# The first projection of an attention and two feed-forward networks in seven block products instead of eight, for the later token tiles

## The chip, the cores and the metric

The kernel runs on one core of a Trainium2 chip. The metric is the device time of one launch in microseconds (us). The core has a matrix engine (TensorE, PE in the rows; its weight loads are PEld), a vector engine (VectorE, DVE), a scalar engine (ScalarE, ACT), a general engine (GpSimd, POOL) and SyncE (SP), which issues most of the transfers here.

## The reference

Three stages follow one another on 6016 tokens with 256 channels.

```
qn = q / |q| over tokens;  kn = k / |k| over tokens
a  = softmax(kn^T qn / tau)                  # 256 x 256, over channels
x  = v a                                     # 6016 x 256
h  = x w_in                                  # 6016 x 2048
g  = h where h >= 1; 0 where h <= -1; (h+1)^2 / 4 between
x  = g w_out                                 # 6016 x 256
xn = x / sqrt(mean(x^2) + 1e-6) * rms_g
y  = (silu(xn w_gate) * (xn w_val)) w_out    # inner width 1536
```

The weights come as 64-bit numbers, the tokens as 32-bit ones, and the output is 32-bit.

## The kernel before

**Precision.** Each operand of the large products is split into a high and a low part (tiles ending in h and l). A product of two blocks of 128 x 128 weights and 128 x 512 tokens is three matmuls: high by high, low by high and high by low.

**Tiles.** The tokens lie in 12 tiles, in six pairs: five pairs of 512 columns a tile and a last one of 448. Tiles stand transposed, channels on the partitions. The attention matrix is folded into the weights: w1 = a w_in is made once (`product_w1`) and kept in SBUF as w1h and w1l.

**First network.** `block_A` makes one block of 128 rows of h for one tile: two halves of the channels by three matmuls, six matmuls into one PSUM bank, 16 blocks a tile. Then come three ScalarE instructions (relu, square, copy to the high part) and two on VectorE (clamp, subtraction to the low part). `block_B` multiplies them by w_out into y, which grows in PSUM over the 16 blocks. `prep_v` turns and splits V for one tile.

**Second network.** `norm` scales x. `combine` makes the seven operands of Strassen's method in Winograd's form from a pair of tiles (two tiles by two channel halves): b11, b21, b22 and the differences t1 to t4. `to_seven` makes the seven weight blocks of a panel, which is two row blocks by two channel halves, and stores them in DRAM; `load_seven` fetches a panel (896 KB). `seven_units` makes the seven products of a panel and a pair, 21 matmuls where the plain way has 24. Its PSUM sum X1 grows over four of the products and is copied out three times on the way (names ending in a, c and u); three VectorE additions complete the sums. `block_D` multiplies by the second w_out.

**Order.** `ORDER` says in which order the networks of the pairs run: first network of pairs 0 and 1, second of pair 0, first of pair 2, second of pair 1, and so on; the second networks of pairs 4 and 5 end it. A string, `CHAIN`, lays out a panel's products (c), those left over from the panel before (t) and the waiting products of the projection that follows (d). A planner written in Python then sorts every operation by a due time, with assumed costs, and gives out buffers by class (`SLOTS`); on each engine the program then keeps that order. Its clock starts where the first block of h is computed, near 62 us on the trace. The transfers are issued from SP's queue in the planner's order too.

Of the kernel before, what the change touches and what calls it, by code (L numbers as in the profile page):

```python
# [62 lines left out]
def tile_channel_attention_two_ffn(  # L63
# [422 lines left out]
    n_op = {cls: SLOTS[cls] for cls in ("stage", "op", "rows")}  # L486
    first_op = {"stage": 0, "op": n_op["stage"], "rows": n_op["op"] + n_op["stage"]}
# [7 lines left out]
    class Buf:  # L495
        def __init__(self, cls, name, shape=None, dtype=F32, slot=None):
            self.cls, self.name, self.shape, self.dtype = cls, name, shape, dtype
            self.slot, self.t, self.users, self.given = slot, None, 0, None
            self.wrote, self.read = {}, {}

# [53 lines left out]
    for t in range(2):  # L554
        V[t] = [Buf("op", f"v{p}{t}", slot=2 * t + i) for i, p in enumerate("hl")]
# [4 lines left out]
    def prep_v(t, at, step):  # L560
        _, n = tiles[t]
        x = Buf("stage", f"vin{t}", [P, NC, TOK])
# [15 lines left out]
    def narrow(key, src, at, step, on_act, into=None):  # L578
        x = Buf("stage", f"wide_{key}", [P, NC, TOK])
# [32 lines left out]
    for p in range(NF2 // 2):  # L612
        kept_dram["wd", p] = drp.tile([P, 4 * C], F32, name=f"kept_wd{p}")
        for nm in "gv":
            kept_dram[nm, p] = drp.tile([P, 2, 7, P], F32, name=f"kept_{nm}{p}")

    def to_rows(kind, j, src, at, step, on_act, eng):
        x = narrow(f"{kind}{j}", src, at, step, on_act)
        w = Buf("rows", f"{kind}{j}", [P, 2, 2, C], F32R)
# [14 lines left out]
    def to_seven(kind, p, src, at, step):  # L634
        f = Buf("stage", f"f{kind}{p}", [P, 8, P])
        h = Buf("stage", f"h{kind}{p}", [P, 7, P], F32R)
        narrow(f"{kind}{p}", src, at, step, True, f)
        for i, (o, a, b, how) in enumerate((
# [9 lines left out]
            at, [(f, s) for s in range(1, 8)], [h], [h])  # L648
# [48 lines left out]
    G, Y = {}, {}  # L697

    def block_A(t, f, at):
        _, n = tiles[t]  # L700
        vh, vl = V[t]
        ps = Buf("mm", f"h{t}_{f}")

        def mm():
# [9 lines left out]
        op("PE", pe(6, n), mm, at, reads, [ps], [ps])  # L714
        r = Buf("tmp", f"g{t}_{f}")
        gh = Buf("tmp", f"gh{t}_{f}", dtype=F32R)
        op("ACT", act(n), lambda: nc.scalar.activation(  # L717
            out=r.t[:, :n], in_=ps.t[:, :n], func=AF.Relu, bias=0.5, scale=0.5),
            at, [ps], [r], [r])
# [3 lines left out]
            out=r.t[:, :n], in0=ps.t[:, :n], scalar=1.0, in1=r.t[:, :n], op0=ALU.max, op1=ALU.min),  # L723
            at, [ps], [r])
        op("ACT", act(n), lambda: nc.scalar.activation(  # L725
            out=gh.t[:, :n], in_=r.t[:, :n], func=AF.Copy), at, [r], [gh], [gh])
        gl = Buf("tmp", f"gl{t}_{f}", dtype=F32R)
# [4 lines left out]
    def block_B(t, f, c, w, at):  # L732
        _, n = tiles[t]
        gh, gl = G[t, f]
        if (f, c) == (0, 0):
# [517 lines left out]
```

## Time and profile before

| what | value |
|---|---|
| median of 3 runs | 1135.0 us (1134.12 to 1135.71) |
| profiled execution, its own time | 1134.83 us |
| its span, first to last instruction | 1133.1 us |
| busy: PE, DVE, ACT, POOL | 1109.2, 820.0, 749.6, 86.4 us |
| bytes moved by DMA | 167.65 MB |

The profile is of one execution. A busy time is the time in which an engine had an instruction under way. Matmuls are pipelined, so the printed durations of neighbours overlap, and what one costs is read from the distance of two starts. The same holds, to a lesser degree, for VectorE and ScalarE.

### The profile page before, as it was taken

Reading aid. Unit: us, or ns where it says so; the run is one execution under the profiler, and the core shown is the slowest. Engines: PE = TensorE matmul, PEld = TensorE weight load, DVE = VectorE, ACT = ScalarE, POOL = GpSimd, SP = SyncE. Lnnn points to the kernel's source line nnn. Section 1 sums busy time; section 2 is a strip of 40 time slices with the busy share of each in tenths; the row PEclk is TensorE's granted clock in tenths of the full one; section 3 lists DMA queues with packets and bytes.
Section 4 is the critical chain, followed back from the end, with each engine's and each line's share of the span. In section 5 each row is a group of like instructions: output and inputs, shape, how many; then the busy total and the mean of one; then the engine's idle time right before and its main releaser. Section 6 shows DMA issues by size and latency. Waiting matters only on the chain.

```text
span 1133.1 us, 13952 instructions
## 1 busy us (share of the span) xinstructions
PE 1109.2 (98%) x4950; PEld 930.7 (82%) x4950; DVE 820.0 (72%) x1311; ACT 749.6 (66%) x1325; POOL 86.4 (8%) x84
## 2 busy tenths in 40 slices
PE   7799999999999999999999999999999999999996
PEld 6678888888888888888888888888888998888995
DVE  5989989969985448886446977445968545976664
ACT  6589898987666666666666556666557566555552
POOL 0000244313100002000000100000200000200000
PEclk9999999999999999999999999999999999999998
DMA  9766575577536413425432432532442412444742
GB/s 346 238 174 180 189 258 217 196 201 260 163 115 185 80 56 135 155 97 123 124 75 102 167 135 53 183 63 89 149 167 103 126 56 92 161 153 155 216 149 33
DMA packets 138854, 167.65 MB, mean 148 GB/s; under 512 B 103712, under 2 KB 103712, under 8 KB 138784
## 3 DMA queue, kind: packets, MB, share of 16 engines
q1 hardware_dynamic: 135072, 166.29, 47.2%
q10 hardware_dynamic: 3712, 0.46, 0.3%
q8 instruction: 39, 0.64, 0.2%
q14 instruction: 31, 0.25, 0.1%
HBM read 142.21 MB, written 24.51 MB: 147 GB/s over the span
## 4 chain that ended last, share of the span: by engine, by line
PE 93%; DMA 4%; DVE 1%; SPq 1%; ACT 0%; issue 0%; DVEq 0%; ACTq 0%
PE y L742 23%; PE h L708 22%; PE o L948 17%; PE vx L855 9%; PE gx L855 9%; PE gy L855 4%; PE vy L855 4%; PE vz L855 2%; PE gz L855 2%; DMA qk<-in_k_dram 1%; DMA wide<-in_moe_w_in_dram 1%; DMA qk<-in_q_dram 1%; PE w_ps L682 1%; SPq L180 1%; DMA soon<-in_moe_w_out_dram 1%; PE w_ps L405 0%
## 5 line engine op out<-in xcount | busy, mean ns | idle before, releaser
L722 DVE SCALAR_TENSOR_TENSOR g<-h,g 128x512 f32<-128x512 f32 (+1 forms) x192 | 129.1, 676 | 144.9 <-ACT g L720 144.9
L742 PE MATMUL y<-gh,wo 128*128 128x512 f32 (+1 forms) x768 | 233.5, 385 | 0.0
L717 ACT ACTIVATE g<-h 128x512 f32<-128x512 f32 (+1 forms) x192 | 112.8, 587 | 121.5 <-PE h L708 121.3
L948 PE MATMUL o<-uh,wd 128*128 128x512 f32 (+1 forms) x576 | 175.6, 386 | 0.0
L742 PEld LDWEIGHTS y<-gh,wo 128*128 128x128 f32 x768 | 144.2, 188 | 27.3 <-DVE wo L143 0.2
L708 PE MATMUL h<-vh,w1h 128*128 128x512 f32 (+1 forms) x384 | 148.1, 386 | 0.3 <-ACT w1h L414 0.3
L708 PE MATMUL h<-vl,w1h 128*128 128x512 f32 (+1 forms) x384 | 148.0, 385 | 0.3 <-DVE vl L143 0.3
L742 PE MATMUL y<-gl,wo 128*128 128x512 f32 (+1 forms) x384 | 148.0, 385 | 0.1
L143 DVE TENSOR_TENSOR gl<-g,gh 128x512 fp32r<-128x512 f32 (+1 forms) x192 | 129.2, 678 | 7.4 <-ACT gh L725 7.1
L948 PEld LDWEIGHTS o<-uh,wd 128*128 128x128 f32 x576 | 108.1, 188 | 20.4
L720 ACT ACTIVATE g<-g 128x512 f32<-128x512 f32 (+1 forms) x192 | 119.0, 621 | 4.2
L725 ACT ACTIVATE gh<-g 128x512 fp32r<-128x512 f32 (+1 forms) x192 | 117.0, 611 | 6.8 <-DVE g L722 6.8
L708 PE MATMUL h<-vh,w1l 128*128 128x512 f32 (+1 forms) x384 | 116.8, 385 | 0.0
L948 PE MATMUL o<-ul,wd 128*128 128x512 f32 (+1 forms) x288 | 111.2, 386 | 1.5 <-DVE ul L143 1.5
L708 PEld LDWEIGHTS h<-vh,w1h 128*128 128x128 f32 x384 | 72.1, 188 | 14.6 <-ACT w1h L414 0.7
L708 PEld LDWEIGHTS h<-vl,w1h 128*128 128x128 f32 x384 | 72.1, 188 | 14.2 <-DVE vl L143 0.6
L742 PEld LDWEIGHTS y<-gl,wo 128*128 128x128 f32 x384 | 72.1, 188 | 13.7 <-DVE gl L143 0.4
L708 PEld LDWEIGHTS h<-vh,w1l 128*128 128x128 f32 x384 | 72.1, 188 | 13.6 <-DVE w1l L415 0.3
L948 PEld LDWEIGHTS o<-ul,wd 128*128 128x128 f32 x288 | 54.1, 188 | 12.1 <-DVE ul L143 1.9
L855 PE MATMUL gy<-xt,gw 128*128 128x512 f32 (+1 forms) x216 | 60.0, 386 | 0.0
L855 PE MATMUL vx<-xt,vw 128*128 128x512 f32 (+1 forms) x216 | 60.0, 386 | 0.0
L855 PE MATMUL gx<-xb,gw 128*128 128x512 f32 (+1 forms) x216 | 60.0, 386 | 0.0
(181 smaller groups left out, 1840.1 us busy)
## 6 DMA issues: line engine op xcount, KB each, us to landing
gw<-kept_g SPq DMA_DIRECT2D x36, 896.0 KB, 4.7
vw<-kept_v SPq DMA_DIRECT2D x36, 896.0 KB, 4.7
wo<-kept_wo SPq DMA_DIRECT2D x40, 512.0 KB, 4.0
wd<-kept_wd SPq DMA_DIRECT2D x36, 512.0 KB, 3.6
vin<-in_v_dram SPq DMA_DIRECT2D x80, 64.0 KB, 3.9
out_dram<-ob SPq DMA_DIRECT2D x80, 64.0 KB, 2.0
qk<-in_q_dram SPq DMA_DIRECT2D x9, 512.0 KB, 10.2
qk<-in_k_dram SPq DMA_DIRECT2D x9, 512.0 KB, 10.2
```

Source lines behind the costliest of these rows:

```text
L143: return eng.tensor_tensor(out=dst_lo, in0=src, in1=hi.bitcast(F32), op=ALU.subtract)
L180: nc.sync.dma_start(out=xv[32 * a:32 * a + 32, c, :n // 32, :], in_=src[a, c])
L682: nc.tensor.matmul(got[b].t, x[:, c * P:(c + 1) * P], w[:, c, :], start=(i == 0), stop=(i == len(terms) - 1),)
L708: nc.tensor.matmul(ps.t[:, :n], w[:, c, f * P:(f + 1) * P], x[:, c, :n], start=(i == 0), stop=(i == len(terms) - 1),)
L717: op("ACT", act(n), lambda: nc.scalar.activation(out=r.t[:, :n], in_=ps.t[:, :n], func=AF.Relu, bias=0.5, scale=0.5), at, [ps], [r], [r])
L720: op("ACT", act(n), lambda: nc.scalar.activation(out=r.t[:, :n], in_=r.t[:, :n], func=AF.Square), at, [], [r])
L722: op("DVE", dve(n), lambda: nc.vector.scalar_tensor_tensor(out=r.t[:, :n], in0=ps.t[:, :n], scalar=1.0, in1=r.t[:, :n], op0=ALU.max, op1=A ...
L725: op("ACT", act(n), lambda: nc.scalar.activation(out=gh.t[:, :n], in_=r.t[:, :n], func=AF.Copy), at, [r], [gh], [gh])
L742: nc.tensor.matmul(y.t[:, c, :n], w.t[:, f % 2, h, cs], x[:, :n], start=(f == 0 and i == 0), stop=(f == NF1 - 1 and i == 2),)
L855: nc.tensor.matmul(ps.t[:, :n], w.t[:, h, a, :], b.t[:, e, :n], start=(start and i == 0), stop=(i == 2), skip_group_check=True,)
L948: nc.tensor.matmul(o.t[:, c, :n], w.t[:, f % 2, h, cs], x[:, :n], start=(nth == 1 and i == 0), stop=(nth == NF2 and i == 2),)
```

## The change

From pair 2 on, the first projection is made by `seven_units` too. Its panels of weights (kind h) are made from w1h + w1l, eight of them, stored in DRAM, and loaded for each pair. V is turned into a plain 32-bit tile and goes through `combine`. The instructions behind a block of h are taken out of `block_A` into `squared`, which reads either PSUM or an SBUF sum. Pairs 0 and 1 stay as they were. The stream class has four buffers in place of three. The class stage is merged into op. CHAIN has another order. The core of the diff:

```diff
-CHAIN = "ccttccddcdd"
-SLOTS = {"mm": 4, "yo": 2, "stage": 7, "op": 19, "rows": 4, "tmp": 20, "seven": 3}
-RESERVE = {"tmp": 4, "mm": 1}
+CHAIN = "cttccdcdcdd"
+CHAIN_1 = "cdttccddcddcddd"
+PLAIN = 2
+H_AT = (70.0, 16.0)
+PREP_S = 50.0
+SLOTS = {"mm": 4, "yo": 2, "op": 24, "rows": 4, "tmp": 20, "seven": 4}
+RESERVE = {"tmp": 4, "mm": 1, "op": 4}
...
-    def to_seven(kind, p, src, at, step):
-        f = Buf("stage", f"f{kind}{p}", [P, 8, P])
-        h = Buf("stage", f"h{kind}{p}", [P, 7, P], F32R)
-        narrow(f"{kind}{p}", src, at, step, True, f)
+    def to_seven(kind, p, at, step, src=None):
+        f = Buf("op", f"f{kind}{p}", [P, 8, P])
+        h = Buf("op", f"h{kind}{p}", [P, 7, P], F32R)
+        if src is not None:
+            narrow(f"{kind}{p}", src, at, step, True, f)
+        else:
+            cols = slice(2 * p * P, 2 * (p + 1) * P)
+            g = 2 * p * P // TOK
+            op("DVE", dve(TOK), lambda: nc.vector.tensor_tensor(
+                out=f.t[:, :4, :].rearrange("p (k s) c -> p k (s c)", k=NC),
+                in0=w1h[:, :, cols].bitcast(F32), in1=w1l[:, :, cols].bitcast(F32), op=ALU.add),
+                at + 2 * step, [(w1_part, (g, c)) for c in range(NC)],
+                [(f, s) for s in range(4)])
...
         op("PE", pe(6, n), mm, at, reads, [ps], [ps])
+        squared(t, f, ps, at)
+
+    def squared(t, f, h, at):
...
-    def combine(q, at, step):
+    def combine(kind, q, x0, x1, at, step):
...
-        w, x = seven[kind, p], XO[q]
+        w, x = seven[kind, p], XO["v" if kind == "h" else "x", q]
...
+    def turn_pair(q, at, step):
+        _, n = tiles[2 * q]
+        raw = []
+        for t in (2 * q, 2 * q + 1):
+            x = Buf("op", f"vin{t}", [P, NC, TOK])
+            r = Buf("op", f"vr{t}", [P, NC, TOK])
+            op("SP", dma(512, 8), lambda x=x, t=t: dma_v(x.t, t), at - LEAD["v"], writes=[x])
+            for c in range(NC):
+                op("DVE", dve(n), lambda c=c, x=x, r=r: nc.vector.transpose(
+                    out=r.t[:, c, :n], in_=x.t[:, c, :n]), at, [x], [(r, c)])
+                at += step
+            raw.append(r)
+        combine("v", q, *raw, at, step)
+
+    def network_1s(q):
+        turn_pair(q, phase_at[1, q] - PREP_S, STEP)
+        n = tiles[2 * q][1]
+        us = pe(3, n)[0]
+
+        def take(p):
+            def made(i, k, d, at):
+                t, f = 2 * q + k, 2 * p + i
+                squared(t, f, d, at)
+                for c in range(NC):
+                    pend.append((us, lambda at, c=c: block_B(t, f, c, rows[p], at)))
+            return made
+
+        rows = {}
+        for p in range(NF1 // 2):
+            load_seven("h", p, now - LEAD["seven"])
+            rows[p] = load_rows("wo", p, now + LEAD["wd"])
+            chain = seven_units("h", q, p, take(p))
+            fill.extend(pend)
+            pend.clear()
+            for what in CHAIN_1:
+                if what == "d":
+                    pop_fill(1)
+                elif what == "t":
+                    if tail:
+                        unit(us, tail.pop(0))
+                else:
+                    unit(us, chain.pop(0))
+            tail.extend(chain)
...
-        (network_1, network_2)[net - 1](q)
+        if net == 2:
+            network_2(q)
+        elif q < PLAIN:
+            network_1(q)
+            if q == 0:
+                for p in range(NF1 // 2):
+                    to_seven("h", p, phase_at[1, PLAIN] - H_AT[0] + H_AT[1] * p, STEP)
+        else:
+            network_1s(q)
```

## Rows read from the trace of the kernel before

**Rows 1.** The page's head: the span, and TensorE's busy time and share.

```profile
span 1133.1 us, 13952 instructions
...
PE 1109.2 (98%) x4950; PEld 930.7 (82%) x4950; DVE 820.0 (72%) x1311; ACT 749.6 (66%) x1325; POOL 86.4 (8%) x84
```

**Rows 2.** TensorE's waits from 72 us on: total us, times, longest.

```profile
PE o L948 <- DVE ul L143: 1.5, 1, 1.5
```

**Rows 3.** Busy times of stretches; at the end granted clock, DMA share, GB/s.

```profile
72.00:170.00 98.00, 98.00 (x434) 81.12 (x433) 93.90 (x160) 89.75 (x163) 19.32 (x22) 1.00 0.67 210
...
244.00:332.00 88.00, 88.00 (x389) 72.79 (x388) 79.04 (x128) 62.48 (x111) 14.16 (x14) 1.00 0.61 194
332.00:420.00 88.00, 88.00 (x390) 72.86 (x389) 47.25 (x74) 56.67 (x98) 0.00 (x0) 1.00 0.40 103
420.00:508.00 88.00, 88.00 (x389) 72.78 (x388) 70.30 (x113) 54.43 (x98) 6.91 (x4) 1.00 0.38 130
```

**Rows 4.** TensorE on the tile h, in one of these stretches: busy (count).

```profile
332.00:420.00 88.00, 48.36 (x192) 1.00 0.40 103
```

**Rows 5.** The chain that ended last, three pieces: start, length, what.

```profile
349.63 1.36 PE h L708 x6
350.99 1.36 PE y L742 x6
...
906.30 1.22 PE h L708 x6
```

**Rows 6.** Timeline from 443 us, TensorE and ScalarE: start, length, instruction.

```profile
443.11 0.63 PE L948 MATMUL o<-uh,wd 128*128 128x512 f32 x2
...
443.31 0.60 ACT L863 ACTIVATE vc<-vx 128x512 f32<-128x512 f32 x1 [0.73 <-PE vx L855]
...
443.80 0.63 ACT L570 ACTIVATE vh<-vt 128x512 fp32r<-128x512 f32 x1
...
444.32 0.62 ACT L912 ACTIVATE gu<-gu 128x512 f32<-128x512 f32 x1
```

**Rows 7.** VectorE's timeline from 292 us: start, length, instruction.

```profile
292.31 0.69 DVE L236 SCALAR_TENSOR_TENSOR fv<-wide_v 128x512 uint32<-128x512 uint32 x1
...
300.55 1.09 DVE L649 TENSOR_TENSOR fv<-fv,hv 128x896 fp32r<-128x896 f32 x1
301.55 0.69 DVE L143 TENSOR_TENSOR vl<-vt,vh 128x512 fp32r<-128x512 f32 x1
...
304.11 0.69 DVE L920 TENSOR_TENSOR s<-s,vx 128x512 f32<-128x512 f32 x1
304.71 1.39 DVE L920 TENSOR_TENSOR vu<-gu,vu 128x512 f32<-128x512 f32 x1
```

**Rows 8.** VectorE from 244 to 332 us by line: count, busy us, mean ns.

```profile
L143 DVE TENSOR_TENSOR xt<-dt,xt 128x512 fp32r<-128x512 f32 x3 | 2.0, 683 | 0.0
...
L143 DVE TENSOR_TENSOR xb<-x,xb 128x512 fp32r<-128x512 f32 x2 | 1.4, 686 | 0.0
...
L824 DVE TENSOR_TENSOR dt<-x,dt 128x512 f32<-128x512 f32 x2 | 1.4, 686 | 0.0
...
L824 DVE TENSOR_TENSOR dt<-x,x 128x512 f32<-128x512 f32 x1 | 0.7, 686 | 0.0
...
L824 DVE TENSOR_TENSOR dt<-x 128x512 f32<-128x512 f32 x1 | 0.7, 682 | 0.0
```

**Rows 9.** SP's timeline, the second store of a panel of w_val.

```profile
301.67 0.32 SPq L655 DMA_DIRECT2D kept_v<-fv  x1
```

**Rows 10.** DMA issues: count, KB each, median us from issue to landing.

```profile
gw<-kept_g SPq DMA_DIRECT2D x36, 896.0 KB, 4.7
...
kept_v<-fv SPq DMA_DIRECT2D x6, 448.0 KB, 3.7
```

**Rows 11.** POOL's timeline, in the stretch of VectorE's rows.

```profile
293.13 2.59 POOL L642 TENSOR_TENSOR fv<-fv 128x128 f32<-128x128 f32 x4 [17.01 <-ACT uh L924]
...
304.23 1.31 POOL L143 TENSOR_TENSOR wd<-wide_wd,wd 128x512 fp32r<-128x512 f32 x1 [8.52 <-ACT wd L621]
```

More of the change, by code (lines that the diff above doesn't have):

```diff
@@ L485, in tile_channel_attention_two_ffn @@
         later_pools[cls] = ctx.enter_context(tc.tile_pool(name=f"{cls}2", bufs=1))
-    n_op = {cls: SLOTS[cls] for cls in ("stage", "op", "rows")}
-    first_op = {"stage": 0, "op": n_op["stage"], "rows": n_op["op"] + n_op["stage"]}
+    first_op = {"op": 0, "rows": SLOTS["op"]}
     at_op = at
@@ L647, in to_seven @@
             out=h.t, in_=f.t[:, 1:, :], func=AF.Copy),
-            at, [(f, s) for s in range(1, 8)], [h], [h])
+            at, [(f, s) for s in range(1, 8)], [h])
         op("DVE", dve(7 * P), lambda: nc.vector.tensor_tensor(
@@ L1013, in tile_channel_attention_two_ffn @@
         late[i] = (phase_at[2, 0] * first + (c[0] - phase_at[2, 0] * first) * (i + 1) / len(late),) + c[1:]
-    for due, _, kind, which, src in [c for c in conversions if c[2] in ("wi", "wo")] + late:
+    rest = [c for c in conversions if c[2] not in ("g", "v", "wd")]
+    for due, _, kind, which, src in sorted(rest + late, key=lambda c: c[:2]):
         at = max(0.0, due - SLACK)
@@ L1022, in tile_channel_attention_two_ffn @@
         else:
-            to_seven(kind, which, src, at, STEP)
+            to_seven(kind, which, at, STEP, src)
     def network_1(q):
@@ L1058, in network_1 @@
             push(*m1.pop(0))
-        for t in ts:
-            last_t[t] = now
-    last_t = {}
+    def turn_pair(q, at, step):
+        _, n = tiles[2 * q]
+        raw = []
+        for t in (2 * q, 2 * q + 1):
+            x = Buf("op", f"vin{t}", [P, NC, TOK])
+            r = Buf("op", f"vr{t}", [P, NC, TOK])
[33 more added lines that the diff above has]
+            tail.extend(chain)
+        while tail:
+            unit(us, tail.pop(0))
+            pop_fill(1)
+        fill.extend(pend)
+        pend.clear()
     def network_2(q):
@@ L1066, in network_2 @@
         at = end_at[1, q] + NORM_AT
-        while fill and (1, q) == before:
-            pop_fill(1)
         for i in range(2):
             norm(2 * q + i, at + i * NORM_GAP, STEP)
-        combine(q, max(at + NORM_GAP + 15 * STEP, phase_at[before] + 8), STEP)
+        combine("x", q, X[2 * q], X[2 * q + 1], max(at + NORM_GAP + 15 * STEP, phase_at[before] + 8), STEP)
         us = pe(3, tiles[2 * q][1])[0]
@@ L1154, in may_start @@
             need[b.cls] = k + 1
-            f = sorted(free[b.cls].values())
+            f = sorted(t for i, t in free[b.cls].items() if b.cls != "mm" or written[i] >= b.seed)
             behind = 0 if queue[b.cls][0] is b else RESERVE.get(b.cls, 99)
@@ L1163, in tile_channel_attention_two_ffn @@
     done = set()
+    written = [0] * SLOTS["mm"]
     front = [o for o in order if o.eng == "PE"]
@@ L1181, in tile_channel_attention_two_ffn @@
                     best = key, o
+        if best is None:
+            print({cls: [(b.name, b.users) for b in {id(b): b for o in ops for b, _, _ in o.uses}.values() if b.cls == cls and b.t is not None and b.users] for cls in SLOTS})
+            print({cls: [b.name for b in q[:3]] for cls, q in queue.items()})
         assert best is not None, [(e, [(o.seq, o.at, [b.name for b in o.new]) for o in p[:4]]) for e, p in pending.items()]
@@ L1192, in tile_channel_attention_two_ffn @@
             f = free[b.cls]
-            b.slot = min((i for i in f if f[i] <= t), key=lambda i: (f[i], i))
+            mm = b.cls == "mm"
+            b.slot = min(
+                (i for i in f if f[i] <= t and not (mm and written[i] < b.seed)),
+                key=lambda i: (mm and written[i], f[i], i),
+            )
             del f[b.slot]
@@ L1196, in tile_channel_attention_two_ffn @@
             b.make()
+            if b.cls == "mm":
+                if not b.seed:
+                    written[b.slot] = b.cols
         clock[o.eng] = t + o.occ
```

47 lines of the change are left out of this document (26 added, 21 removed).

## The prediction

> **What bounds the kernel now.** I read the page's head first, then the waits of TensorE, then the stretches, then single instructions. TensorE is busy for 1109.2 of 1133.1 us [rows 1]. From 72 us on it waits once, 1.5 us, in the last few microseconds of work [rows 2]. In every stretch that I cut by stage its busy time equals the stretch [rows 3]. The other columns of the same rows say how near the other engines are: VectorE 93.90 of 98 us and ScalarE 89.75 in the first stretch, 79.04 of 88 and 62.48 in the stretch of the first pair's second network (244 to 332), 47.25 and 56.67 in the first network of pair 2 (332 to 420), 70.30 and 54.43 in the second network after it. So TensorE sets the time, by its count of matmuls, and the reader should carry away that VectorE at 96% did not make it wait. What a change is worth here is the matmuls it removes, less every wait that it puts into TensorE's order. I call the first and second network of pair q (1,q) and (2,q).
>
> **What is removed.** The tile h has 192 matmuls in the window of (1,2) [rows 4]: 16 column blocks, two tiles, six each. Seven products per group of two blocks and two tiles, three matmuls each, are 8 x 21 = 168, so 24 fewer per pair. Six matmuls take 1.36 us from start to start on 512 columns and 1.22 on 448 [rows 5], 0.2267 and 0.2033 each. Pairs 2 to 4 give 3 x 24 x 0.2267 = 16.3 us, pair 5 gives 24 x 0.2033 = 4.9. Sum: **-21.2 us**. The second projection (y) keeps its number of matmuls and so does the second network.
>
> **What is added inside a streamed phase, and what hides it.** Each of the 8 groups gets three copies out of PSUM on ScalarE and three adds on VectorE, as the g and v products have them. An instruction's printed duration overlaps its neighbour, so I price by spacing: a copy of PSUM is followed 0.49 us later by the next instruction and one from SBUF 0.52 later [rows 6]; VectorE's two-input operations stand 0.60 apart [rows 7]. 24 copies at 0.52 are 12.5 us, 24 adds 14.4. The phase shrinks from 88 to 88 - 8 x 0.68 = 82.6 us. ScalarE: 56.67 + 12.5 = 69.2 of 82.6 (84%). VectorE: 47.25 + 14.4 = 61.7 (75%). Both are below the 92% and 96% of the first stretch in [rows 3], which cost TensorE nothing. I take nothing for this; were the cover gone, 12.5 us per phase would be the worst, 50 us in all.
>
> **The operands.** The old preparation of V is four transposes, four copies and four subtractions for a pair. The new one has four transposes, four differences and seven copy-and-subtract parts: 3 more on ScalarE, 7 more on VectorE, in the second network before. That is 7 x 0.60 = 4.2 us on VectorE: 74.5 of 88 in the window of (2,1), hidden. Its 16 loads of V keep their lead (50 + 20 us ahead), so no queue position changes for them.
>
> **The panels.** Eight conversions, each one VectorE add (0.60), four POOL operations, one ScalarE copy of 896, one VectorE subtraction of 896 (1.00 to the next instruction, [rows 7]), and two stores on SP. On the planner's clock they start at 202 us, 16 apart; its zero is near 62 on the trace, so at 264, 280, 296, 312, then 328 to 376, and about 4.4 of them fall into (2,0), where VectorE has only 88 - 79.04 = 9.0 us free. Added there: 4.4 x 1.6 = 7.0, plus 4.2 for the operands, 11.2 in all, 2.2 too many. But nine operations in that window (xt, xb and dt, [rows 8]) belong to the combination for (2,1); the code asks for them 8 us into (1,2), and they were taken early because VectorE was idle. Nine at 0.60 are 5.4 us that slide back into (1,2), which has room (61.7 + 5.4 + 3.6 x 1.6 = 72.9 of 82.6). Nothing taken; uncovered it costs 2.2 us, once.
>
> Is the last panel there in time? Panel 7 starts at 376. In the trace a panel of w_val goes from its join at 292.31 [rows 7] to the issue of its second store at 301.67 [rows 9], 9.4 us; the store lands after 3.7 us, the load after 4.7 [rows 10]. With two steps of 1.5 us ahead of the add that is 376 + 3 + 9.4 + 8.4 = 397. Group 7 starts at 332 + 7 x 10.2 = 403 (45 matmuls per group). Slack 6 us, the thinnest in the change. Past it TensorE waits on the transfer, and SP's queue behind the load (rows of w_out, then the next panels) waits too.
>
> **Transfers.** Eight loads of 896 KB per phase are 7.3 MB more; (1,2) now moves 103 GB/s x 88 us = 9.1 MB. 16.4 MB in 82.6 us is 199 GB/s, and the first stretch carried 210 with TensorE full [rows 3]. The fourth stream buffer lets one more load run ahead. Nothing taken, and I allow no gain either: no load is waited for now.
>
> **PSUM handoffs.** The product sum X1 is copied three times a group while it grows, and each copy must end before the next product adds to it. In [rows 6] TensorE went on to other work at 443.11, the copy began at 443.31 and lasted 0.60: free 0.80 after. The new order for the first projection leaves at least four products (2.7 us) between such steps. The new order for the second network narrows one gap, from four products to three (2.0 us), as wide as the two others there already are. Each is above 0.80. Nothing taken.
>
> **One rule against the change.** The row: VectorE's operation at 304.71 lasts 1.39 us instead of 0.69 [rows 7], and a POOL operation runs from 304.23 to 305.54 [rows 11]; yet this operation and the four of a panel from 293.13 lie in the stretch of (2,0), in which TensorE never waited [rows 2]. The Trainium skill, page "SBUF — State Buffer", section "SBUF: two separate sides", says that a VectorE operation with two SBUF inputs and a POOL operation that reads SBUF lock each other out for a whole instruction. The change adds 32 POOL operations, and the adds and many squares now have two SBUF inputs. By that rule the sum would be the third rival's, without it mine.
>
> **Sum.** The profiled execution took 1134.83 us, 1.7 more than its span, and lies 0.2 below the median of 1135.0. 1134.83 - 21.2 = 1113.6. For small waits where the new orders meet I add 0.7, half of the only wait that the old order has [rows 2]; its bounds are -1.5 (that wait vanishes) and the rivals' prices. **1114.3 us.** By itself this case lies between 1112.0 and 1116.5.
>
> **Rivals.**
> 1. *Panel 7, or the crowd in (2,0), comes late.* For: 6 us of slack, and VectorE at 90% before 11.2 us are added. Against: planned order with work that can slide. If all of 11.2 arrives uncovered at one place less the 9.0 that are free, and the panel slips by as much as its slack again, 2.2 + 6 = 8.2 us are lost: 1116 to 1122.
> 2. *ScalarE becomes the bound in the streamed phases.* It then has 120 block instructions and, at worst, 7 of a combination. By spacing (0.52) 66 us, by the longest printed duration in [rows 6] (0.63) 80 of 82.6 us. The phase has nothing in hand at the second price; 2 us lost in each of four phases give 1114.3 + 8 = 1122.
> 3. *POOL blocks VectorE.* 32 operations at 1.39 - 0.69 = 0.70 are 22.4 us, of which 4.4 x 4 x 0.70 = 12.3 in (2,0): 11.2 + 12.3 - 9.0 - 5.4 = 9.1 us late, 1123.
> 4. *Slower: the copies of X1 come late at every step.* 4 pairs x 8 groups x 3 = 96 handoffs; 21.2 / 96 = 0.22 us of wait at each cancels the gain. The copy has 2.7 us and needs 0.80, so it must start 2.1 us late, behind four more ScalarE instructions of 0.52, each time. Five behind it would cost 0.7 x 96 = 67 us: 1181. Against: 72 such groups (36 g, 36 v) run now without a wait [rows 2]. For: ScalarE at 84%, not 62%.
> 5. *The removed matmuls are not missed*, because loads of panels set the pace: each group needs 896 + 512 KB in 10.2 us, 138 GB/s, and 4.7 us to land; only if SP's queue stood still for over 16 us at each group would this give 1135.
>
> **How the numbers follow.** Forecast 0.70; rival 1 0.11; rival 2 0.07; rival 3 0.05; rival 4 0.05; rival 5 0.02. The range must leave out at most 0.2: 1112.0 (no wait, the old one gone) to 1122.0 takes in the forecast with rivals 1 and 2. Within 0.2% (2.3 us) a measurement of this kernel cannot tell a change. Slower 0.04 is rival 4 beyond its point of balance; the hundredth of it that stays short of that point goes to faster, which is 0.70 + 0.11 + 0.07 + 0.05 + 0.01 = 0.94; the same 0.02 is rival 5.
>
> **What would show it.** After the change TensorE should have 96 matmuls fewer, and the stretches of (1,2) to (1,5) should be full at some 82 us. The tile h should be written by the line of the seven products. ScalarE near 84% and VectorE near 75% in these stretches show the second paragraph of costs right. A wait of TensorE on a DMA of a kept h panel near 395 to 410 us shows rival 1, waits of products on ScalarE's copies rivals 2 or 4, VectorE adds of over 1 us beside POOL rival 3. I would be wrong if TensorE's order, now with fewer matmuls between a product and its use, is denser in waits than the one row of before lets me see.

## The result, and the profile after

The changed kernel takes 1122.2 us (median of 4, 1121.87 to 1123.61) against 1134.6 (1134.12 to 1135.71): ratio 0.9892, 95% interval 0.9875 to 0.9909. It is faster, as forecast, but by 12.4 us, where the forecast took 20.7 off the 1135.0 that it had; the range ended 0.2 us short of the result. The head of the page of the profile after:

```profile
span 1120.0 us, 14173 instructions
...
PE 1091.8 (97%) x4854; PEld 913.9 (82%) x4854; DVE 913.0 (82%) x1451; ACT 799.3 (71%) x1441; POOL 104.3 (9%) x116
```

Against [rows 1] that is 96 matmuls fewer. Where the rest went is seen in TensorE's waits from 72 us on (total, times, longest), against the single row of [rows 2]:

```profile
PE o L969 <- DVE ul L147: 2.5, 2, 1.6
PE o L969 <- DVE ob L980: 2.4, 1, 2.4
PE y L762 <- ACT x L769: 1.7, 2, 0.9
PE hy L876 <- DVE s L941: 0.6, 1, 0.6
```

And by stretch (columns as in [rows 3]; the last are granted clock, DMA share and GB/s):

```profile
242.00:300.00 58.00, 58.00 (x257) 47.88 (x256) 53.26 (x84) 41.57 (x72) 13.51 (x16) 1.00 0.51 170
300.00:320.00 20.00, 20.00 (x90) 16.36 (x89) 19.71 (x32) 14.93 (x27) 3.53 (x5) 1.00 0.62 214
320.00:340.00 20.00, 19.30 (x84) 15.30 (x82) 20.00 (x30) 14.59 (x26) 7.56 (x9) 1.00 0.82 280
340.00:360.00 20.00, 16.19 (x63) 12.87 (x64) 18.51 (x31) 13.31 (x24) 6.54 (x8) 0.91 0.71 176
414.00:502.00 88.00, 87.15 (x385) 71.76 (x384) 74.40 (x120) 56.73 (x103) 6.58 (x4) 1.00 0.45 151
506.00:587.00 81.00, 81.00 (x359) 67.08 (x358) 59.46 (x95) 63.60 (x117) 0.00 (x0) 1.00 0.61 173
```

Most of it is lost in one place, where (2,0) ends and (1,2) begins: VectorE is busy 20.00 of 20 us and TensorE misses 0.7 and then 3.8. Elsewhere in these rows TensorE is full, but for 0.85 in the stretch of (2,1). Taken as whole stages, (2,0) and (1,2) leave VectorE room, 5.0 us of 90 and 14.6 of 82; it is full only where they meet:

```profile
242.00:332.00 90.00, 90.00 (x397) 74.17 (x396) 84.97 (x133) 66.43 (x115) 23.24 (x28) 1.00 0.56 190
332.00:414.00 82.00, 77.49 (x332) 62.99 (x332) 67.40 (x105) 64.47 (x116) 10.44 (x14) 0.98 0.77 233
```

TensorE's timeline at the place:

```profile
333.63 0.84 PE L876 MATMUL hx<-vt,hw 128*128 128x512 f32 x3
335.05 0.96 PE L876 MATMUL hy<-vt,hw 128*128 128x512 f32 x3 [0.57 <-DVE s L941]
...
339.26 0.61 PE L969 MATMUL o<-uh,wd 128*128 128x512 f32 x2
341.45 0.50 PE L969 MATMUL o<-ul,wd 128*128 128x512 f32 x1 [1.58 <-DVE ul L147]
...
342.94 0.39 PE L969 MATMUL o<-ul,wd 128*128 128x512 f32 x1
345.69 0.73 PE L969 MATMUL o<-uh,wd 128*128 128x512 f32 x2 [2.36 <-DVE ob L980]
346.26 0.40 PE L969 MATMUL o<-ul,wd 128*128 128x512 f32 x1
346.49 2.34 PE L876 MATMUL hx<-vb,hw 128*128 128x512 f32 x6
348.63 1.05 PE L762 MATMUL y<-gh,wo 128*128 128x512 f32 x2
```

I measure a loss as the distance of two matmul starts beyond the regular 0.2267 us. The three waits make 0.74, 1.74 and 2.52. Then six matmuls take 2.14 us from start to start (346.49 to 348.63) where [rows 5] has 1.36: the granted clock is 0.91 in the stretch, TensorE runs at the lower of its two levels for eight matmuls, and that costs 1.6 more. **Lost at the boundary: 6.6 us.** Over the whole trace, from the first matmul of h to the last matmul (61.59 to 1110.60, before 62.57 to 1124.07), such losses add to 12.2 us against 3.9 before (of which less than 2 lie ahead of 72 us in either). I call this sum the lost time below (some expectations call it excess), and quote it for every run. From first to last matmul it is 1061.5 us before and 1049.0 after, 12.5 less: some 20.8 of matmuls gone, 8.3 of lost time come in.

What VectorE does there, from its timeline (start, length):

```profile
330.44 0.95 DVE L147 TENSOR_TENSOR ul<-va,uh 128x512 fp32r<-128x512 f32 x1
331.31 1.82 DVE L147 TENSOR_TENSOR xb<-x,xb 128x512 fp32r<-128x512 f32 x2
333.05 1.34 DVE L664 TENSOR_TENSOR fh<-fh,hh 128x896 fp32r<-128x896 f32 x1
...
337.31 1.08 DVE L664 TENSOR_TENSOR fh<-fh,hh 128x896 fp32r<-128x896 f32 x1
...
340.72 0.68 DVE L147 TENSOR_TENSOR ul<-vc,uh 128x512 fp32r<-128x512 f32 x1
341.32 0.68 DVE L844 TENSOR_TENSOR dxt<-x,dxt 128x512 f32<-128x512 f32 x1
341.92 0.68 DVE L648 TENSOR_TENSOR fh<-w1h,w1l 128x512 f32<-128x512 f32 x1
342.53 0.68 DVE L147 TENSOR_TENSOR xt<-dxt,xt 128x512 fp32r<-128x512 f32 x1
343.13 0.68 DVE L742 SCALAR_TENSOR_TENSOR g<-hu,g 128x512 f32<-128x512 f32 x1
343.73 0.68 DVE L147 TENSOR_TENSOR gl<-g,gh 128x512 fp32r<-128x512 f32 x1
344.33 0.68 DVE L147 TENSOR_TENSOR xt<-dxt,xt 128x512 fp32r<-128x512 f32 x1
344.93 2.50 DVE L980 STREAM_TRANSPOSE ob<-o 128x512 f32<-128x512 f32 x4
```

Three things are to be seen. The combination for (2,1) (xb, dxt, xt) has slid back, but not far enough: its first operation starts at 331.31 (before, at 317.63), and six of its eleven operations still lie between 331 and 345 us, ahead of the last hand-offs of (2,0). Panel work (fh) stands between them. And the transposes ob, for which TensorE waits from 343.3 on, are seventh in line behind the ul that released TensorE at 341.45. Beside POOL's differences (four from 329.99 to 333.44) the operations last 0.95 us each (two of them are merged in the row of 1.82) and 1.34 us, where they take 0.68 and 1.08 alone.

The two waits on x are a smaller case. TensorE's rows and ScalarE's, at 438 us:

```profile
437.90 0.84 PE L876 MATMUL gx<-xt,gw 128*128 128x512 f32 x3
439.60 0.73 PE L762 MATMUL y<-gh,wo 128*128 128x512 f32 x2 [0.85 <-ACT x L769]
```

```profile
438.96 0.59 ACT L769 ACTIVATE x<-y 128x512 f32<-128x512 f32 x1
```

In the new order a product stands between the last matmuls on the two halves of y, so the copy out of the first half comes ahead of the last matmuls on the second, in the same PSUM tile, and TensorE waits until it has been read. Twice 1.01 us.

### The profile page after: what moved, and what is told of

Read it like the earlier page. It is cut to its first block, busy times and chain, and to the rows that moved or that the text cites. A ratio compares the mean times of both kernels' runs of the same rounds, so it can differ in the third digit from the quotient of the medians.

```text
span 1120.0 us, 14173 instructions
## 1 busy us (share of the span) xinstructions
PE 1091.8 (97%) x4854; PEld 913.9 (82%) x4854; DVE 913.0 (82%) x1451; ACT 799.3 (71%) x1441; POOL 104.3 (9%) x116
## 4 chain that ended last, share of the span: by engine, by line
PE 90%; DMA 4%; DVE 3%; SPq 1%; ACT 1%; issue 0%; DVEq 0%; ACTq 0%
PE y L762 23%; PE o L969 16%; PE vx L876 8%; PE gx L876 8%; PE hx L876 7%; PE h L724 7%; PE gy L876 4%; PE vy L876 4%; PE hy L876 4%; PE gz L876 2%; PE vz L876 2%; PE hz L876 2%; DMA qk<-in_q_dram 1%; DMA wide<-in_moe_w_in_dram 1%; DMA qk<-in_k_dram 1%; PE w_ps L697 1%
## 5 line engine op out<-in xcount | busy, mean ns | idle before, releaser
L147 DVE TENSOR_TENSOR gl<-g,gh 128x512 fp32r<-128x512 f32 (+1 forms) x192 | 132.7, 701 | 10.8 <-ACT gh L745 10.8
L762 PEld LDWEIGHTS y<-gl,wo 128*128 128x128 f32 x384 | 72.2, 188 | 14.1 <-DVE gl L147 0.4
L876 PE MATMUL vx<-xb,vw 128*128 128x512 f32 (+1 forms) x216 | 59.9, 386 | 0.0
L876 PE MATMUL gx<-xt,gw 128*128 128x512 f32 (+1 forms) x216 | 59.8, 385 | 0.0
L876 PE MATMUL vy<-xt,vw 128*128 128x512 f32 (+1 forms) x216 | 59.8, 385 | 0.0
L809 POOL TENSOR_SCALAR m<-sb 128x16 f32<-128x16 f32 (+1 forms) x12 | 4.9, 408 | 583.5 <-DVE sb L807 583.1
L889 DVE TENSOR_TENSOR hc<-hy,hc 128x512 f32<-128x512 f32 (+1 forms) x32 | 21.4, 670 | 39.9 <-PE hy L876 39.9
L876 PE MATMUL hy<-vt,hw 128*128 128x512 f32 (+1 forms) x192 | 53.3, 386 | 0.6 <-DVE s L941 0.6
L876 PE MATMUL hx<-vt,hw 128*128 128x512 f32 (+1 forms) x192 | 52.9, 384 | 0.0
L876 PE MATMUL hx<-vb,hw 128*128 128x512 f32 (+1 forms) x192 | 52.6, 389 | 0.0
```

Source lines behind the costliest of these rows:

```text
L147: return eng.tensor_tensor(out=dst_lo, in0=src, in1=hi.bitcast(F32), op=ALU.subtract)
L762: nc.tensor.matmul(y.t[:, c, :n], w.t[:, f % 2, h, cs], x[:, :n], start=(nth == 1 and i == 0), stop=(nth == NF1 and i == 2),)
L809: nxt("POOL", pool(0.3), lambda: nc.gpsimd.tensor_scalar(out=m.t[:, :nb], in0=s1.t[:, :n].rearrange("p (b j) -> p b j", j=32)[:, :, 0], sc ...
L876: nc.tensor.matmul(ps.t[:, :n], w.t[:, h, a, :], b.t[:, e, :n], start=(start and i == 0), stop=(i == 2), skip_group_check=True,)
L889: op("DVE", dve(n), lambda: nc.vector.tensor_tensor(out=d.t[:, :n], in0=b.t[:, :n], in1=d.t[:, :n], op=ALU.add), at, [b], [d], urgent=20)
```

## The experiments

Each ratio is to runs of the kernel before on the same chip, in brackets its 95% interval. The edits are to the changed kernel. A caution holds for all edits but two (e13 and e14): the planner sees an edit and sorts anew, so the waits move.

**The changed kernel again** (e7, no edit).

> The changed kernel once more, unaltered, beside the others of this set. Every theory expects the ratio of its first measurement, 0.989 (0.9875 to 0.991), so some 12 us off the kernel before, and again about 6.6 us lost where the second network of pair 0 meets the first network of pair 2. If that loss jumped by more than 1 us between two runs of the same program, differences of that size between the experiments would mean nothing.

0.990 [0.9885, 0.9914], lost time 12.0, at the boundary 0.76, 0.45, 1.13, 2.52 and 1.6 at the lower clock. It repeats itself.

**No panels (e1).** The loads fetch stored panels of w_gate instead.

```diff
+        src = ("g", p % (NF2 // 2)) if kind == "h" else (kind, p)
-            out=w.t.bitcast(F32), in_=kept_dram[kind, p]),
+            out=w.t.bitcast(F32), in_=kept_dram[src]),
...
-                    to_seven("h", p, phase_at[1, PLAIN] - H_AT[0] + H_AT[1] * p, STEP)
```

> Left out: the conversion of the h panels; each phase loads the stored w_gate panels in their place, so the first projection of pairs 2 to 5 uses other weights, with the same instructions, loads and matmuls. Theory A (VectorE is too full around the end of (2,0): the panels' adds and subtractions, 8 x 1.6 = 13 us, make the last products of that phase late): the three waits of 0.74, 1.74 and 2.52 us near 334 to 343 and the slow clock after them (1.6 us) go, 1122.2 - 6.6 = 1115.6 us. Theory C (the loss sits in the streamed phases themselves, in handoffs and loads): no panels conversions matter little, 1120 to 1122. Theory B (POOL's additions block VectorE) also gives 1116, since they go too; the next two runs part A from B.

0.984 [0.9825, 0.9855], lost time 4.9, nothing over 0.17 us at the boundary. So the streamed stages, their loads, copies and additions cost next to nothing (one of the two waits on x is still there, 1.0 us): the loss at the boundary comes with making the panels.

**Streamed from pair 3 on (e5); and the same with early panels (e10).** The second puts the panels into the first network of pair 2, and has e4's edit.

```diff
-PLAIN = 2
+PLAIN = 3
```

> The seven products start one pair later, from pair 3 on. That removes 72 matmuls instead of 96: 2 x 24 x 0.2267 + 24 x 0.2033 = 15.8 us. The panels of h are then made in the second network of pair 1, where VectorE was busy 70.3 of 88 us before the change, so 17.7 us are free for some 11 of new work. Crowd theory (VectorE had no room in the second network of pair 0): the loss at the boundary goes, and what stays is about 1.5 us of small waits, so -14.3 us, ratio near 0.9875, a little better than the changed kernel although fewer matmuls are removed. Rival (each streamed first network costs its share, wherever the panels are made): the 12.4 us gained shrink in proportion to the matmuls, to 9.3, ratio near 0.992.

0.9886 [0.9869, 0.9902]. The boundary is without loss, lost time 4.8; a wait of 1.4 us on gl stays at 525 us. The trace is 14.65 us shorter than before, first h to last matmul, where 14.3 was expected; the median fell by 13.0. A quarter fewer matmuls are removed and as much time is won.

```diff
-H_AT = (70.0, 16.0)
+H_AT = (170.0, 11.0)
```

> The seven products start from pair 3 on, the panels are made in the first network of pair 2, which then stays as it was before the change (VectorE 47.25 of 88 us busy), and the copy waits for both halves of y. Crowd theory: 15.8 us of matmuls go and nothing new is lost; from the first matmul of h to the last one the trace is 15.8 us shorter than before (1061.5), within 0.5, and the ratio is 0.986 to 0.9875. Rival (the second network of pair 1 loses time by itself): the wait of 1.4 us near 525 us stays, ratio 0.9885.

0.9883 [0.9867, 0.9900]. The wait at 525 us is gone and the lost time is 4.3, near that of before. Yet the trace is only 14.0 us shorter, not 15.8: this kernel's matmuls on 448 columns run at the slower spacing in two stages, those of the kernel before in one (last section), some 1.2 us. The theory holds for the waits; the time expected from it did not come.

**POOL's differences twice (e2); VectorE's panel addition twice (e3).** Each is the operation issued two times for a panel of h.

```diff
+            for _ in range(2 if src is None else 1):
                 op("POOL", pool(0.7), lambda o=o, a=a, b=b, how=how: nc.gpsimd.tensor_tensor(
```

> Each of the 32 POOL additions of the h panels is done twice, with the same result. Theory B: VectorE is lengthened by 32 more blocks of up to 0.3 to 0.7 us, a third to a half of them in the crowded 40 us, so 3 to 7 us more: 1125 to 1129. Theory A: POOL is not what is full; each panel is some 3 us later but is awaited with slack, 1121 to 1124.

0.9932 [0.9915, 0.9948], lost time 14.1. VectorE's 512-column operations from 242 to 365 us last 6.7 us in all beyond 0.70 each; in the changed kernel 3.1, before about 1. The 1125.4 us are at the low end of theory B's range and above theory A's.

```diff
+            for _ in range(2):
                 op("DVE", dve(TOK), lambda: nc.vector.tensor_tensor(
                     out=f.t[:, :4, :].rearrange("p (k s) c -> p k (s c)", k=NC),
```

> The VectorE addition that opens each h panel is done twice, with the same result: 8 x 0.60 = 4.8 us more on VectorE, none on POOL. Theory A: up to 4.8 us more waiting, 1125 to 1128. Theory B: 1122 to 1123.

0.9911 [0.9897, 0.9926], lost time 13.0. The boundary's waits shrink in the new order and one of 2.7 us on a load of hw appears at 399 us. It is the seventh panel's load, not the last one's, for which the prediction counted 6 us of slack: SP issued that panel's second store and then its load behind eight loads of V each (382.33 to 389.4 and 391.12 to 396.9 us), and the load landed at 402.1. The 1123.2 us miss theory A's range (1125 to 1128) and lie just above theory B's: the added work was not paid in the crowd.

**The panels' subtraction on POOL (e6).**

```diff
-        op("DVE", dve(7 * P), lambda: nc.vector.tensor_tensor(
+        eng, cost = (nc.vector, dve(7 * P)) if src is not None else (nc.gpsimd, pool(2.8))
+        op("DVE" if src is not None else "POOL", cost, lambda: eng.tensor_tensor(
```

> The subtraction of 896 columns of each of the eight h panels runs on POOL instead of VectorE. That takes some 1.0 us off VectorE at each, about 5 of them in the second network of pair 0 and the start of the next stage. Crowd theory: the 6.6 us lost at the boundary shrink to 2 to 4, ratio 0.985 to 0.987. Rival (POOL beside VectorE is what lengthens VectorE's work): eight more and longer POOL operations with SBUF inputs give back what is taken off, boundary loss 6 us or more, ratio 0.989 to 0.993.

0.9946 [0.9931, 0.9961], lost time 16.3: the rival, by more than it had asked. Taking work off VectorE made VectorE later. POOL's subtractions and VectorE's operations beside them, in this kernel:

```profile
334.58 2.12 POOL L665 TENSOR_TENSOR fh<-fh,hh 128x896 fp32r<-128x896 f32 x1
...
340.70 2.58 POOL L665 TENSOR_TENSOR fh<-fh,hh 128x896 fp32r<-128x896 f32 x1
```

```profile
334.22 0.68 DVE L890 TENSOR_TENSOR vu<-vy,vu 128x512 f32<-128x512 f32 x1
334.82 2.42 DVE L845 TENSOR_TENSOR dxt<-x,dxt 128x512 f32<-128x512 f32 x1
337.16 0.94 DVE L942 TENSOR_TENSOR vu<-gu,vu 128x512 f32<-128x512 f32 x1
...
341.22 2.62 DVE L147 TENSOR_TENSOR ul<-vu,uh 128x512 fp32r<-128x512 f32 x1
```

A VectorE operation with two SBUF inputs that starts while POOL subtracts ends some 0.55 us after POOL does, as if its own work began only then: 2.42 and 2.62 us instead of 0.68. Beside a later subtraction (364.21 to 366.89) an addition that reads PSUM (hc, 365.25) keeps its 0.69, and the next operation, with two SBUF inputs (gl, 365.86), lasts 1.58. The Trainium skill, page "SBUF — State Buffer", section "SBUF: two separate sides", says that the engine that starts first keeps the shared pair of ports for the whole instruction; here the trace agrees.

**The differences left out (e11).** ScalarE copies four blocks in their place.

```diff
+        if src is None:
+            op("ACT", act(TOK), lambda: nc.scalar.activation(
+                out=f.t[:, 4:, :], in_=f.t[:, :4, :], func=AF.Copy),
...
-        )):
+        ) if src is not None else ()):
```

> The four POOL differences of each h panel are left out, and ScalarE fills the four blocks with a copy of the first four, so the weights of the first projection are other ones. VectorE's own work, the loads and the matmuls stay. Theory that POOL's operations lengthen VectorE's beside them: the 3.1 us that VectorE's 512-column operations last beyond 0.70 us between 242 and 365 us fall below 1.5, and the 6.6 us lost at the boundary fall to 2 to 4, ratio 0.986 to 0.988. Theory that it is VectorE's added work alone: the loss stays at 5 to 6.6, ratio 0.989 to 0.990.

0.9854 [0.9839, 0.9868], lost time 6.7, at the boundary 1.1, less than the theory's 2 to 4. But VectorE's order is another one here too, so this does not yet tell POOL from order.

**Two runs with every engine's order unchanged (e13, e14).** In the first POOL fills instead of subtracting, in the second VectorE's subtraction is cut to one block in seven.

```diff
-                in0=f.t[:, a, :], in1=f.t[:, b, :], op=how),
+                in0=f.t[:, a, :], in1=f.t[:, b, :], op=how) if src is not None else nc.gpsimd.memset(f.t[:, o, :], 0.01),
```

> The order of instructions on every engine is that of the changed kernel. POOL's four differences of each h panel become fills with a constant, of the same size and in the same places, which read nothing; the weights of the first projection are other ones. Lock theory (a POOL operation with SBUF inputs lengthens VectorE's two-input operations beside it): the 3.1 us beyond 0.70 us of VectorE's operations between 242 and 365 us fall to about 1, and the loss at the boundary falls from 6.6 to 2 to 4 us, ratio 0.986 to 0.988. Theory that VectorE's own added work is the whole cause: nothing changes, 0.989 to 0.990, loss 6 to 7 us.

0.9877 [0.9862, 0.9891], lost time 8.9. The boundary has 0.23, 0.88 and 2.50 and no matmul at the lower clock. VectorE beside the fills, POOL first:

```profile
324.12 1.81 POOL L658 MEMSET fh<- 128x128 f32 x12
```

```profile
325.26 0.68 DVE L648 TENSOR_TENSOR fh<-w1h,w1l 128x512 f32<-128x512 f32 x1
325.86 0.68 DVE L147 TENSOR_TENSOR ul<-vu,uh 128x512 fp32r<-128x512 f32 x1
```

They keep their 0.60 from start to start, and VectorE's lengthening between 242 and 365 us falls from 3.1 to some 1.4 us. The fills are also shorter than the differences, so reading and length are not told apart; but POOL's differences, and no order, made 1.4 us of the waits. The other 1.6 of the 3.0 us that went are the lower clock. Whether it left with the differences is not shown: three executions of e13 took 1118.7 to 1119.2 us, a fourth 1121.2 with a lower mean clock (0.993, the others 0.994 and 0.995).

```diff
-            out=f.t[:, 1:, :].bitcast(F32R), in0=f.t[:, 1:, :], in1=h.t.bitcast(F32),
+        lo = 1 if src is not None else 7
+        op("DVE", dve(7 * P), lambda: nc.vector.tensor_tensor(out=f.t[:, lo:, :].bitcast(F32R), in0=f.t[:, lo:, :],
+            in1=h.t[:, lo - 1:].bitcast(F32), op=ALU.subtract), at + step, [h], [(f, s) for s in range(1, 8)])
```

> The order of instructions on every engine is that of the changed kernel. VectorE's subtraction of each h panel covers 128 columns instead of 896 (the low parts of six of the seven blocks are left unsubtracted), some 0.8 us less on VectorE at each, of which three lie between 330 and 349 us. Theory of VectorE's own work: 2.4 us off just ahead of the late operations and more before them, so the boundary loss falls from 6.6 to below 3, ratio 0.985 to 0.987. Lock theory alone: POOL's operations still lengthen VectorE's, loss 5 us or more, ratio 0.988 to 0.990.

0.9891 [0.9876, 0.9906], lost time 10.7: 0.18, 0.64 and 2.52 at the boundary, and the lower clock is back. Waits 1.7 us shorter in the trace, the ratio the same within its interval. Both theories had a part, and both missed: the longest wait did not move in either run, 2.50 and 2.52. The stretch from 340 to 360 us in e13 and then in e14, with the granted clock:

```profile
340.00:360.00 20.00, 17.65 (x76) 14.30 (x77) 19.85 (x33) 14.88 (x27) 0.00 (x0) 1.00 0.77 194
```

```profile
340.00:360.00 20.00, 17.17 (x68) 13.33 (x67) 17.70 (x31) 13.24 (x24) 6.54 (x8) 0.91 0.79 201
```

The trace of e14 is of an execution of 1122.4 us at a mean clock of 0.992; another of the same program took 1118.7 at 0.995, as quick as e13's best. So the lower clock may come in some executions of a program and not in others, and one trace of each does not settle it.

**Who stands ahead of the transposes (e17, e8, e15).** First the transposes of the first half of o wait for both halves, except in the last pair.

```diff
-                out=ob.t[:, :n], in_=o.t[:, c, :n]), at, [(o, c)], [ob], [ob], urgent=20)
+                out=ob.t[:, :n], in_=o.t[:, c, :n]), at,
+                [(o, 0), (o, 1)] if t // 2 < NPAIR - 1 else [(o, c)], [ob], [ob], urgent=20)
```

> The transposes of the first half of o are made to wait for the last matmuls on both halves (not in the last pair), so in program order no matmul on the tile stands behind them. Theory of the tile's order: the wait on ob (2.3 us, gap 2.5) is gone, the rest of the boundary's waits stay or shift (1 to 3 us, with or without 1.6 us at the lower clock), ratio 0.986 to 0.988. Rival (VectorE is so late that the next thing that TensorE needs of it comes late by the same 2 us): another wait takes its place, boundary loss 5 us or more, ratio 0.989 or above.

0.9862 [0.9845, 0.9878], lost time 8.3. The ratio is the theory's, the rows lean to the rival: the wait of 2.4 is gone, and others of 1.0 and 0.95 took its place (the two gaps add to 2.28 us, the one was 2.52):

```profile
346.01 0.74 PE L969 MATMUL o<-uh,wd 128*128 128x512 f32 x2 [1.00 <-DVE ob L980]
...
349.32 0.70 PE L762 MATMUL y<-gh,wo 128*128 128x512 f32 x2 [0.95 <-ACT g L738]
```

VectorE's order is that of the changed kernel up to 346 us. Boundary 4.7 with no matmul at the lower clock (1.6 of the gain); the rest is the two waits on x (2.0), which this order happens not to have, and faster 448-column matmuls (1.2).

Next the combination, asked for later, by 36 us and by 48.

```diff
-        combine("x", q, X[2 * q], X[2 * q + 1], max(at + NORM_GAP + 15 * STEP, phase_at[before] + 8), STEP)
+        combine("x", q, X[2 * q], X[2 * q + 1], max(at + NORM_GAP + 15 * STEP, phase_at[before] + 36), STEP)
```

> The combination of the next pair's operands is asked for 36 us after the start of the first network before it, not 8, so that its nine VectorE operations stand behind the hand-off at the boundary. The prediction had them slide back there by themselves (5.4 us). Crowd theory: with them gone from the crowd 5 of the 6.6 us lost at the boundary return, ratio near 0.985, if the operands are still there when the second network of that pair starts. Rival (the crowd is the panels' own work and its POOL operations, not the combination's): boundary loss stays near 6 us, ratio 0.988 to 0.990. If the operands come too late instead, TensorE waits for them at the start of the second networks of pairs 1 to 3, on the tiles of the combination, and the ratio is above 0.990.

0.9887 [0.9872, 0.9901], lost time 10.1, at the boundary 3.9 without the lower clock: 2.7 of the expected 5 came back, 1.1 of them in waits and 1.6 through the clock, and the ratio stayed in the rival's range. The wait on ob is 1.38 long, not 2.52.

> Only the second edit of e9: the combination is asked for 48 us into the stage before it, the copy waits for one half of y as in the changed kernel. If e9's gain (ratio 0.9842 against 0.990) is the combination moved out of the crowd, the ratio is 0.984 to 0.986, with two waits of 0.85 us on the copy back in the trace. If the copy's edit carried it, the ratio stays near e8's, 0.9885.

0.9869 [0.9852, 0.9885], lost time 9.0, boundary 2.8: between the theory's ratio and e8's. One of the two waits on x is back, and 1.1 us of the gain is the faster spacing of 448-column matmuls. So a part of e9's gain (below) is here; e9 loses 2.7 us less, of which 1.0 is that wait and 1.2 is at the boundary.

**The copy out of y after both halves (e4); with the combination 48 us late (e9); with e17's edit as well (e18).**

```diff
-                at, [(y, 0)], [(x, 0)], [x], urgent=20)
+                at, [(y, 0), (y, 1)], [(x, 0)], [x], urgent=20)
```

> ScalarE's copy of the first half of y is placed only when both halves are complete. Theory D (the waits of 1.0 us at 438 and 611 come from that copy standing in the program ahead of the last matmuls on the other half of the same tile, so these wait for a read that doesn't concern them): both waits go, 2.0 us, 1120.2. Rival: the copy is itself the late thing, then y is freed later and the second network's first output tile waits in their place: 1122 to 1123. The order around (2,0) may move by itself, by some 1 us either way.

0.9888 [0.9874, 0.9903], lost time 8.9: the waits on x are gone, as theory D had it, and the boundary has 3.9 in five waits in another order. The ratio does not stand clear of the changed kernel's 0.9892 and 0.990.

> Two edits that each took off little are put together: the copy out of the first projection's sum waits for both halves of y, and the combination of the next pair is asked for 48 us into the stage before it. If their losses are separate (1.0 us at each of two copies, and the share of the nine VectorE operations at the boundary), the ratio goes to 0.986 to 0.988. Rival: both only relieve the same place, VectorE around 340 us, and together give no more than each alone, 0.9885 to 0.989.

**0.9842 [0.9828, 0.9857], 1116.3 us**, lost time 6.3: three small waits at the boundary (1.6 in all), none on x. Better than either expectation; 1.1 us of it is again the faster spacing of 448-column matmuls.

> e9 (copy after both halves of y, combination asked for 48 us into the stage before it) and e17's transposes after both halves of o. If the three take away waits of their own, the waits on ob of e9 (0.3 us at the boundary and three of about 0.3 us in the later second networks) go too, and the ratio is 0.983 to 0.984, with an excess over regular spacing below 5.5 us. Rival (re-sorting moves VectorE's work to another hand-off, as in the earlier runs): the ratio is 0.985 or above, worse than e9's 0.9842.

0.9846 [0.9831, 0.9861], 1115.8 us, lost time 5.2. Lost time as the theory had it, ratio not better than e9's; its last second network runs at the slower 448-column spacing, 1.2 us. These two beat both kernels, and the runs do not tell them apart.

**Two parts of the change undone (e12, e16).** Three stream buffers:

```diff
-SLOTS = {"mm": 4, "yo": 2, "op": 24, "rows": 4, "tmp": 20, "seven": 4}
+SLOTS = {"mm": 4, "yo": 2, "op": 24, "rows": 4, "tmp": 20, "seven": 3}
```

> The stream class has three buffers again, as before the change; all else is the changed kernel. By the prediction's part on transfers no load is waited for, so nothing changes: ratio 0.989 to 0.990, no wait of TensorE on a DMA. Rival (the fourth buffer carries part of the gain): TensorE waits on loads of hw, gw or vw in each of the four streamed first networks, 1 us or more each, ratio above 0.993.

0.9949 [0.993, 0.9968], lost time 17.7. The ratio is the rival's, the rows are not: TensorE waits 4.1 us once, at 338.9, on a load of wd, not of hw, and 2.5 us at 353 on ScalarE, each with matmuls at the lower clock behind it. SP's queue, of this kernel and then of the changed one:

```profile
334.87 0.32 SPq L683 DMA_DIRECT2D hw<-kept_h  x1
336.66 0.32 SPq L670 DMA_DIRECT2D kept_h<-fh  x1
337.02 0.43 SPq L676 DMA_DIRECT2D wd<-kept_wd  x1
```

```profile
325.66 0.32 SPq L683 DMA_DIRECT2D hw<-kept_h  x1
...
331.01 0.38 SPq L676 DMA_DIRECT2D wd<-kept_wd  x1
```

The loads stand in one line. With three buffers hw's is issued 9.2 us later, and the load of wd behind it 6.0 us later. Some 1.1 us of both is a later start of the whole (first h at 62.73, not 61.59). SP's waits fit a wait for a free buffer: hw's issue was released by a product of the second network (PE vy), after 2.1 us.

The order of the second networks:

```diff
-CHAIN = "cttccdcdcdd"
+CHAIN = "ccttccddcdd"
```

> The order of products in the second networks is the one from before the change; all else is the changed kernel. The prediction gave the new order no price and no gain. If so, the ratio is 0.989 to 0.990 and the waits at the boundary are of the same kind. Rival (the new order narrows a gap between product and copy and so makes the waits): the waits on VectorE's sums at the boundary shrink by more than 2 us, ratio below 0.9875. Rival on the other side (the new order is needed): more waits in all five second networks, ratio above 0.992.

0.9921 [0.9906, 0.9936], lost time 13.3, the boundary alike with more and smaller waits. The ratio just passes the second rival's 0.992, but there are not more waits in all five second networks. The new order is worth at most a little here (1.1 us by the trace, and the ratios' intervals overlap), and does not make the loss.

## Why the prediction was right in sign and wrong in size

*What is removed* stands: 96 matmuls, and the regular spacings sum to 20.8 us less (forecast 21.2). *Inside a streamed phase* stands, in (1,3) (506 to 587 us): ScalarE 63.60 of 81 us (79%, forecast 84), VectorE 59.46 (73%, forecast 75), TensorE full, no wait on a product's copy. *The operands* stand: VectorE 74.40 of 88 us in (2,1), forecast 74.5. Rivals 2, 4 and 5 are out by the same rows and by e1.

**The step that failed is "The panels"**: "Nine at 0.60 are 5.4 us that slide back into (1,2) ... Nothing taken; uncovered it costs 2.2 us, once." It weighed sums over whole stages, and by these there was room: VectorE is busy 84.97 of 90 us up to 332 and 67.40 of 82 in (1,2), where the prediction had 72.9. The loss is made where the stages meet, in a queue that is full for some 40 us. Its three errors:
- The combination slid, but not behind the hand-offs. Its due time, 8 us into (1,2), sorts it ahead of the last hand-offs of (2,0), the transposes at 345. Asked for later, it gave back 2.7 us (e8) and, 48 us late, 3.8 (e15), 1.6 of either through the clock.
- POOL's operations were priced at nothing here, as they cost TensorE nothing in [rows 11]. There VectorE had 9.0 us of slack in the stage. In the crowd they cost TensorE 1.4 us of waits (e13). Rival 3 overpriced them: from 242 to 365 us they lengthened VectorE's operations by some 2 us (3.1 against 1.0 before), not 12.3; an operation that a 128-column difference lengthens mostly takes 0.95 us, 0.27 longer, not 0.70, and many beside one keep their 0.68.
- The longest wait was set by the queue, not by the sum of the work. Six operations ahead of the transposes, 3.6 us, held TensorE 2.4 us; shortening other work left that wait as it was (e13, e14), moving the combination away cut it from 2.52 to 1.38 (e8, e15).

Of 6.6 us, 1.6 are the lower clock after the waits, for which the prediction had no term. Rival 1 (0.11) names the right place and its price, 8.2 us, is near; but it put 6 of them on panel 7, which came in time in the changed kernel. It landed at 402.9, 2.3 us ahead of its first product, so the slack was thinner than the 6 us stated, but not through the making of the panel, which was in DRAM by 380.9: its load stood on SP's queue behind 16 loads of V (383.9 to 397.7), which the count of the slack left out.

**The small waits** ("I add 0.7") were undersized: 2.0 us for the copies out of y. "PSUM handoffs" weighed how soon X1 is copied, and not that y's two halves share a tile. In the other direction the tail's gap fell from 1.66 to 1.06 us. 6.6 + 2.0 - 0.6 and some tenths make the 8.3 us.

**"Transfers"** ("Nothing taken, and I allow no gain either") held for the sum but not for its reason: without the fourth buffer some 6 us more are lost (e12).

What stays open: how the 6.6 us split exactly, since e13 and e14 each took a part and their sum was not run; and what brings the lower clock, which was in one of these two traces and may change from one execution to the next.

## What to carry to other kernels

When work is added to a nearly full engine, look past the sum for the stage: list what stands in that engine's queue ahead of the last hand-off of the stage, and give work that is not yet needed a later due time. Do not move work from VectorE to POOL in a stage where VectorE is full (e6). Where two halves share a PSUM tile, try the read of the first behind the last write of the second: for the copies out of y the waits went (e4), for the transposes the wait moved elsewhere (e17).

## What the hardware showed that was not expected

**TensorE's lower clock after small waits.** Waits of 0.74, 1.74 and 2.52 us between 334 and 346 us were followed by eight matmuls at 0.427 us from start to start, the 1.2 GHz level; so were 0.18, 0.64 and 2.52 (e14). In e3 a single wait of 2.7 us had eight behind it. After 0.23, 0.88 and 2.50 in the trace of e13 none was. The lengths of the waits do not tell them apart.

**Two spacings for the same matmul.** Matmuls on 448 columns stand 0.2027 us apart in some stages and 0.2067 in others (means over 20 us), all products of a stage alike, at a granted clock of 1.00. The stretch from 1040 to 1080 us, second network of the last pair, in the changed kernel and in e18 (TensorE's count is the third number):

```profile
1040.00:1080.00 40.00, 40.00 (x199) 37.01 (x198) 26.55 (x46) 21.89 (x43) 0.00 (x0) 1.00 0.65 198
```

```profile
1040.00:1080.00 40.00, 40.00 (x196) 36.32 (x195) 25.20 (x42) 21.06 (x42) 0.00 (x0) 1.00 0.55 184
```

It is worth 1.1 to 1.3 us for each of the last pair's two stages. The kernel before and e18 have the larger spacing in (2,5), the changed kernel in (1,5), in both its traces; e8, e9, e15 and e17 in neither stage, e10 in both. So before and after compare alike, and 1.1 us of what e8, e9, e15 and e17 gain over the changed kernel is not their edits' work on the waits. The cause was not tried. It limits what the ratios can tell: 0.1%.
